# A streamed decode kernel: 256 more kept floats of W_q, a shorter weight ring in six places, eight loads fewer

## The chip, the cores and the metric

The kernel runs on one core of a Trainium2 chip. The metric is the time of one execution on the device in microseconds (us). A core has TensorE (PE, matmuls, its weight loads shown apart as PEld), VectorE (DVE), ScalarE (ACT), GpSimd (POOL) and SyncE (SP), which here does little else than issue the loads. Sixteen DMA engines move the data; every load from SP is cut by partition rows and spread over them.

## The reference

Two layers with the same weights, each of them an attention block and a gated block, on four tokens with 640 features:

```
W = 1024                                   # only the last 1024 cached positions
q = (layernorm(x) @ wq) in 32 heads of 128
p = softmax(q . k_cache[:, :, -W:] * 128**-0.5)
x = x + (p . v_cache[:, :, -W:]) @ wo
gate, up = layernorm(x) @ W_gate, layernorm(x) @ W_up      # 640 -> 1728
x = x + ((gate * (gate > 0)) * up) @ W_down
# all of it twice, the second time from the x of the first
```

All is float32. A layer reads about 168 MB of weights and cache (329,024 floats a partition).

## The kernel before, in words

**Data.** The host lays everything out as rows over 128 partitions. A size in this text is in floats a partition, so one unit is 512 bytes of a load over all partitions. There are four sources: `heads` (W_q, K, V and W_o of heads 0 to 26, in the order of use), `kept` (the same for heads 27 to 31, the groups K0 and K1), `mlp` (25,920 floats: W_gate, W_up and W_down) and `limbs` (512 columns of V of head 17, cut into pieces with few rows).

**Memory.** One big tile, `store`, has `STORE` floats a partition; beside it `first_q` holds the first `HELD` floats of `heads` from the start of the program to layer two, which so needn't load them again. In most of a layer the heads run through three places of `MOST` floats in `store` (`stretch`). Near the end of layer one `kept` fills the first `FRONT` = 47,360 floats, and its K, V, W_q and W_o stay there for layer two. Layer one's `mlp` has to pass through what is left: `f` (from `FRONT` to the end of `store`), and `a`, `k`, `q` (`AHEAD`, `BACK`, `AWAY`), which are parts of `kept` or of layer two's place that are moved away for that time: into `probs`, the two `pT` tiles and PSUM. The list `gu` says in which place each piece of `mlp` goes; this is the ring.

**Order.** `plan` is the list of all loads. `load()` issues from its front as long as the place of the next load is free (`live`); `done` and `free` mark places as free once the PE products that read them, or the copies that move them, are in the program. So all loads go through SP's one queue in a fixed order, and a load whose place isn't free yet holds up all that follow it. Limbs are loaded by L238 five or fewer rows at a time into the last `PART` floats of `store`.

**Computing.** Per layer: `normalized` and `deviation` (layer norm), then for each group of heads `query`, `scores`, `softmax`, `values`, `project`, where each product is one call of `product` (L276); then `forward`, which computes the gated block in the pieces `gate(j)`, `gated(j)`, `down(j)`. `busy(n)` and `fill(n)` (L358, L365) put products on PE whose results nobody reads; they do so only while `waits[0]` is true, and `normalized` sets it.

Of the kernel before, what the change touches and what calls it, by code (L numbers as in the profile page):

```python
# [13 lines left out]
B, D, H, DH, W, F = 4, 640, 32, 128, 1024, 1728  # L14
P = 128
# [11 lines left out]
KV = 4096  # L27
# [3 lines left out]
K0, K1 = N - 2, N - 1  # L31
KEPT = len(HEADS[K0]) + len(HEADS[K1])
# [25 lines left out]

HELD = 4608
STORE = 50304
FRONT = KEPT * 2 * (D + KV)


AHEAD = KEPT * D, KEPT * D + 1088
INSIDE = 864
BACK = FRONT - 2 * KV - 1728, FRONT - 2 * KV
AWAY = BACK[0] - 1280, BACK[0]
HOME = 12864  # L70
FIRST, MOST = 32128, 16064
LAP = 3 * MOST
SPLIT, PART = 17, 2048
LIMBS = [(half + i, 5, 0, 1536) for i in range(4) for half in (0, 32)] + [(i, 2, 1536, PART) for i in range(3)] + [(3, 1, 1536, PART), (7, 1, 1536, PART)]
RUNS = [(half, 20, 512 * s, 40 * s + 20 * (half > 0)) for s in range(3) for half in (0, 32)] + [(0, 8, 1536, 120)]


# [36 lines left out]
def decode_kernel(ctx: ExitStack, tc: tile.TileContext, x, source, out):  # L114
# [29 lines left out]
    def stretch(layer, lo, end, to):  # L144

        loads = []
        for hi in fewest(lo, end, -(-(end - lo) // MOST))[1]:
            if to + hi - lo > LAP:
                to = 0
            loads.append((lo, hi, to))  # L150
            to, lo = to + hi - lo, hi
        last = next(i for i, (lo, hi, _) in enumerate(loads) if lo < at_part("v", SPLIT) + KV - 512 <= hi)
        for i, (lo, hi, at) in enumerate(loads):
            if last - 3 < i <= last:
                half = (i - last + 1) * 6 + 1
                plan.extend((layer, "limbs", p, p + 1, STORE - PART) for p in range(max(half, 0), half + 6))
            put(layer, "heads", at, lo, hi)
        return to

# [16 lines left out]
    assert to <= KEPT * D or to > 2 * MOST, to  # L176
    put(0, "kept", KEPT * D, KEPT * D, q_end)
    put(0, "heads", q_end, turn, *mid, heads_end)
    put(0, "kept", k0, k0, k1, v0, v0 + 6656, v1, v1 + KV, v1 + 7168, FRONT)
    put(0, "kept", 0, 0, len(HEADS[K0]) * D, KEPT * D)  # L180


    f, z, a, q, k = FRONT, STORE - D, AHEAD[0], AWAY[0], BACK[0]
    assert STORE - FRONT == 1280 + 1024 + D
    gu = [(z, D), (f, 1280), (f + 1280, 1024), (a, 1088), (k, 960), (k + 960, 768), (q, 1280)]
    gu_end = [(f, 1280), (f + 1280, 1024), (z, D), (a, D + 256)]
    wd = [(k, 960), (k + 960, D), (q, 1280), *gu_end, (k, D), (k + D, D)]
    lo = 0
    for to, n in gu + gu + gu_end + wd:
        put(0, "mlp", to, lo, lo + n)  # L190
        lo += n
    assert lo == MLP


    lo = HELD
    for to, n in (f, 1280), (f + 1280, 1024), (z, D), (a, 1088), (k, 1728):
        put(1, "heads", to, lo, lo + n)
        lo += n
    to = AHEAD[1]
    for n in 832, 1280, 1024, 2048, 3392:  # L200
        to = put(1, "heads", to, lo, lo + n)
        lo += n
    assert to == HOME
# [47 lines left out]
    def place(layer, row, lo):  # L251

        if row == "heads" and lo < HELD:
            return first_q, lo, HELD - lo
        most = KV
        if row == "kept" and layer:
            if AHEAD[0] <= lo < AHEAD[1]:
                i = lo - AHEAD[0] - INSIDE
                if i < 0:
                    return probs, 1024 + i, -i  # L260
                return pT[i // P], GAP + i % P, min(P - i % P, AHEAD[1] - lo)
            if BACK[0] <= lo < BACK[1]:
                return store, HOME + lo - BACK[0], BACK[1] - lo
            most = min(x - lo for x in (AHEAD[0], BACK[0], FRONT) if x > lo)
        for first, m, p in held[key(layer, row)]:
            if first <= lo < first + m:
                return store, p + lo - first, min(first + m - lo, most)
        raise KeyError((layer, row, lo))
# [105 lines left out]
            nc.tensor.matmul(m[32 * g:32 * g + 32], sel_q, a, start=True, stop=True, tile_position=(0, 32 * g))  # L374
        return m

    def normalized():

        ysb, xc, sq = probs[:, :QUARTER], gates[:, :QUARTER], gates[:, QUARTER:2 * QUARTER]
        waits[0] = True  # L380
        nc.vector.tensor_reduce(su, y, axis=AX.X, op=ALU.add)
        nc.scalar.copy(ysb, y)
        busy(2)
        mu = mean(su)
        nc.vector.tensor_tensor(xc, ysb, mu.to_broadcast([P, QUARTER]), op=ALU.subtract)
# [77 lines left out]
    def values(layer, g, last=False):  # L463
# [30 lines left out]
        if last:  # L494
            waits[0] = layer == 0
            fill(1, pp[:, 0])
            nc.vector.tensor_copy(gates[:, 2 * P:], po[:, 2 * P:])  # L497
            nc.scalar.copy(gates[:, :2 * P], po[:, :2 * P])
            if layer == 0:
                nc.gpsimd.tensor_copy(pT[0][:, GAP:], store[:, AHEAD[0] + INSIDE:AHEAD[0] + INSIDE + P])  # L500
                rest = AHEAD[1] - AHEAD[0] - INSIDE - P
                nc.vector.tensor_copy(pT[1][:, GAP:GAP + rest], store[:, AHEAD[1] - rest:AHEAD[1]])
# [31 lines left out]

    def attention(layer):
        gs = order[layer]
        rstd = deviation(normalized())
        table(AF.Exp)
        query(layer, gs[0], True)
        if layer:  # L540
            for t in pT:
                nc.gpsimd.memset(t, 0.0)
        query_out(gs[0], rstd)
        query(layer, gs[1])
# [8 lines left out]
        for before, g, after, then in zip([None] + gs, gs, gs[1:] + [None], gs[2:] + [None] * 2):  # L553
            totals(g)
            turned()
            if layer == 0 and after is None:
                nc.scalar.copy(probs[:, QUARTER:], store[:, AHEAD[0]:AHEAD[0] + INSIDE])
                nc.scalar.copy(ps.rearrange("p j n -> p (j n)"), store[:, BACK[0]:BACK[0] + 1024])
                nc.scalar.copy(yy[:, QUARTER:3 * QUARTER], store[:, BACK[1] - 320:BACK[1]])
            if before is not None:  # L560
                values_turned(before)
            if then is not None and before is not None:
                query(layer, then)
                query_out(then, rstd)
# [18 lines left out]
        project(layer, gs[-1], True)  # L583

    def forward(layer):
        ss = normalized()
        gus, hTs = {}, {}

        def gate(j):
# [145 lines left out]
```

## Time and profile before

| | before |
|---|---|
| time, median of 3 runs | 729.77 us (729.51 to 730.13) |
| the profiled execution's own time | 729.74 us |
| its span, first to last instruction | 727.9 us |
| PE busy, DVE busy, ACT busy | 62%, 10%, 7% of the span |
| loads issued by SP | 93 (26 of them limbs) |
| bytes moved by the loads' queue | 310.37 MB in 13,392 packets |
| mean rate over the span | 427 GB/s |
| mean granted clock of TensorE | 0.815 of 2.4 GHz |

The profiled execution's time is 1.84 us more than its span; that part lies outside the instructions. The share of DMA is the mean over the sixteen engines, so 1.00 says that all of them had a packet under way all the time (packets overlap a little, so values just over 1 occur). The granted clock of PE has two levels, 1.2 and 2.4 GHz, shown as 0.50 and 1.00.

### The profile page before, as it was taken

Reading aid. Unit: us, or ns where it says so; the run is one execution under the profiler, and the core shown is the slowest. Engines: PE = TensorE matmul, PEld = TensorE weight load, DVE = VectorE, ACT = ScalarE, POOL = GpSimd, SP = SyncE. Lnnn points to the kernel's source line nnn. Section 1 sums busy time; section 2 is a strip of 40 time slices with the busy share of each in tenths; the row PEclk is TensorE's granted clock in tenths of the full one; section 3 lists DMA queues with packets and bytes.
Section 4 is the critical chain, followed back from the end, with each engine's and each line's share of the span. In section 5 each row is a group of like instructions: output and inputs, shape, how many; then the busy total and the mean of one; then the engine's idle time right before and its main releaser. Section 6 shows DMA issues by size and latency. Waiting matters only on the chain.

```text
span 727.9 us, 8368 instructions
## 1 busy us (share of the span) xinstructions
PE 450.0 (62%) x3824; PEld 146.9 (20%) x3824; DVE 70.5 (10%) x217; ACT 54.5 (7%) x102; POOL 2.4 (0%) x14
## 2 busy tenths in 40 slices
PE   3546565654645574619868896475756556558576
PEld 1111111111111121103334241021211012102123
DVE  2010001000010000001111211000000010001011
ACT  2000000000000000000412210000000000000100
POOL 0000000000000000000000000000000000000000
PEclk9567888887777787759999999677777878769989
DMA  9999999999999999999999999999999999999997
GB/s 409 444 394 447 440 444 434 412 435 444 443 428 416 421 457 418 444 422 426 418 414 412 426 431 452 429 441 433 434 423 440 438 436 417 441 444 423 425 420 312
DMA packets 13442, 310.91 MB, mean 427 GB/s; under 512 B 1576, under 2 KB 1916, under 8 KB 7136
## 3 DMA queue, kind: packets, MB, share of 16 engines
q1 hardware_dynamic: 13392, 310.37, 99.2%
q8 instruction: 30, 0.49, 0.2%
q14 instruction: 4, 0.03, 0.0%
q10 hardware_dynamic: 16, 0.01, 0.0%
HBM read 310.32 MB, written 0.05 MB: 426 GB/s over the span
## 4 chain that ended last, share of the span: by engine, by line
DMA 77%; PE 20%; DVE 1%; issue 1%; SPq 1%; ACT 0%; DVEq 0%; ACTq 0%
DMA store<-in_heads 62%; DMA store<-in_kept 9%; PE ps L276 8%; DMA store<-in_mlp 6%; PE po L276 6%; PE m L276 2%; PE y L276 1%; PE pp L276 1%; PE pp L461 1%; PE po L490 0%; PE m L432 0%; SPq L238 0%; PE po L358 0%; PE m L521 0%; PE m L512 0%
## 5 line engine op out<-in xcount | busy, mean ns | idle before, releaser
L276 PE MATMUL po<-store,pT 128*16 128x512 f32 x1026 | 157.9, 711 | 120.9 <-DMA store<-in_heads 115.2
L276 PE MATMUL ps<-store,qT 128*4 128x512 f32 (+2 forms) x998 | 152.7, 698 | 101.0 <-DMA store<-in_heads 80.7
L276 PEld LDWEIGHTS po<-store,pT 128*16 128x16 f32 x1026 | 33.4, 109 | 229.5 <-DMA store<-in_heads 126.7
L276 PEld LDWEIGHTS ps<-store,qT 128*4 128x4 f32 x998 | 30.8, 94 | 204.3 <-DMA store<-in_heads 91.8
L457 ACT ACTIVATE probs<-ps,nm 128x1024 f32<-128x1024 f32 x17 | 18.9, 1113 | 334.6 <-DVE nm L453 334.6
L453 DVE TENSOR_REDUCE nm<-ps 128x1 f32<-128x1024 f32 x17 | 20.8, 1225 | 233.9 <-PE ps L276 233.9
L276 PE MATMUL m<-store,xT 128*32 128x512 f32 (+3 forms) x146 | 27.9, 580 | 20.8 <-DMA store<-in_heads 20.8
L276 PE MATMUL y<-store,oT 128*4 128x160 f32 x512 | 23.2, 313 | 10.2 <-DMA store<-in_heads 8.9
L508 ACT COPY gates<-po 128x512 f32<-128x512 f32 x16 | 9.4, 586 | 256.5 <-PE po L276 256.5
L276 PE MATMUL pp<-store,xT 128*32 128x256 f32 (+2 forms) x320 | 20.3, 351 | 9.2 <-DMA store<-in_mlp 4.7
L470 DVE COPY pT<-pp 128x32 f32<-128x32 f32 x64 | 10.3, 184 | 143.5 <-PE po L276 126.4
L461 PE MATMUL pp<-sel_sb,probs 128*128 128x128 f32 x144 | 21.3, 297 | 0.0
L461 PEld LDWEIGHTS pp<-sel_sb,probs 128*128 128x128 f32 x144 | 18.7, 156 | 0.0
L514 DVE RECIPROCAL r<-m 128x16 f32<-128x16 f32 x18 | 4.6, 257 | 123.5 <-PE m L512 123.5
L276 PEld LDWEIGHTS y<-store,oT 128*4 128x4 f32 x512 | 12.7, 89 | 18.4 <-DMA store<-in_heads 9.2
L425 DVE TENSOR_SCALAR gates<-m,rstd 128x512 f32<-128x512 f32 (+2 forms) x18 | 12.4, 690 | 27.1 <-PE m L276 27.1
L276 PEld LDWEIGHTS pp<-store,xT 128*32 128x32 f32 x320 | 10.4, 109 | 17.7 <-DMA store<-in_mlp 8.5
L432 PE MATMUL m<-sel_sb,gates 128*128 128x128 f32 x64 | 12.7, 324 | 0.3 <-DVE gates L425 0.3
L276 PEld LDWEIGHTS m<-store,xT 128*32 128x32 f32 x146 | 6.0, 113 | 32.4 <-DMA store<-in_heads 23.3
L521 PE MATMUL m<-sel_sb,gates 128*128 128x128 f32 x72 | 11.9, 288 | 0.8 <-DVE gates L497 0.8
L432 PEld LDWEIGHTS m<-sel_sb,gates 128*128 128x128 f32 x64 | 7.9, 160 | 19.7 <-issue 18.9
L276 PE MATMUL y<-store,gates 128*4 128x160 f32 (+2 forms) x188 | 9.8, 296 | 1.7 <-DMA store<-in_mlp 1.1
(91 smaller groups left out, 135.7 us busy)
## 6 DMA issues: line engine op xcount, KB each, us to landing
store<-in_heads SPq DMA_DIRECT2D x15, 7936.0 KB
store<-in_heads SPq DMA_DIRECT2D x6, 8032.0 KB
store<-in_heads SPq DMA_DIRECT2D x2, 8000.0 KB
store<-in_heads SPq DMA_DIRECT2D x1, 7872.0 KB
store<-in_heads SPq DMA_DIRECT2D x1, 7424.0 KB
store<-in_heads SPq DMA_DIRECT2D x1, 7360.0 KB
store<-in_heads SPq DMA_DIRECT2D x1, 7168.0 KB
store<-in_heads SPq DMA_DIRECT2D x1, 6400.0 KB
```

The costliest lines, as they stand in the source:

```text
L276: nc.tensor.matmul(out[:, a:z], by, t[rows, p:p + z - a], start=start and not a, stop=stop and z == n, **how)
L425: nc.vector.tensor_scalar(gates[:, :len(HEADS[g]) * P], qp.pop(g), rstd, SCALE, op0=ALU.mult, op1=ALU.mult)
L432: nc.tensor.transpose(qt[:, i], gates[:, i * P:(i + 1) * P], ident)
L453: nc.vector.tensor_reduce(nm[g], to.rearrange("p j n -> p (j n)"), axis=AX.X, op=ALU.max, negate=True)
L457: nc.scalar.activation(probs, sc.pop(g).rearrange("p j n -> p (j n)"), AF.Exp, bias=nm.pop(g), accum_out=sums[g])
L461: nc.tensor.transpose(pp[:, c // 4, c % 4 * P:c % 4 * P + P], probs[:, c * P:(c + 1) * P], ident)
L470: nc.vector.tensor_copy(to, pp.rearrange("p j (c x) -> p (j c) x", c=4)[:, :, i:P:32])
L508: nc.scalar.copy(gates, po)
L514: nc.vector.reciprocal(r[g], so.rearrange("p (b i) -> p i b", b=B)[:, :SIDE])
L521: nc.tensor.transpose(ot[:, 127 * b:127 * b + P], gates[:, b * P:(b + 1) * P], ident)
```

## The change

- `HELD` grows from 4608 to 4864 floats: 256 more floats of W_q stay in `first_q` for layer two and are not loaded a second time. `STORE` shrinks by the same 256, to 50,048, and with it `MOST`, from 16,064 to 16,000.
- The ring of layer one's `mlp` is cut anew: 1280, 1408, 1152, 960, 768 and 1280 (6848 floats in six places) instead of 640, 1280, 1024, 1088, 960, 768 and 1280 (7040 in seven). The `mlp` takes 23 loads instead of 27, and layer two's first loads into the same places are four instead of five.
- `AHEAD` grows by 64 floats. What is moved out of it no longer fits in `probs` and the two `pT`: the last 32 floats go into `qT`, by a copy on POOL, and POOL clears `qT` as well in layer two before it's used again. The copy on DVE into the second `pT` is 128 floats wide instead of 96.
- The W_o of the kept heads comes in one load of 3200 instead of 1920 and 1280, and two of the kept V loads are 6144 and 6144 instead of 6656 and 5632.
- The limbs of a layer come in 12 loads instead of 13: the last 512 columns in four loads of two rows, instead of three of two and two of one. Six stand ahead of the load that brings head 17's V and six ahead of the load before that one; they were spread as 1, 6 and 6 over the last three such loads before.
- `normalized` gets an argument. The unread products are left out in the first layer norm of layer one and the second of layer two: in each of the two `busy(2)` and `fill(1)`, six products in all.

```diff
-HELD = 4608
-STORE = 50304
+HELD = 4864
+STORE = 50048
-AHEAD = KEPT * D, KEPT * D + 1088
+AHEAD = KEPT * D, KEPT * D + 1152
-FIRST, MOST = 32128, 16064
+FIRST, MOST = 32000, 16000
...
-            if last - 3 < i <= last:
-                half = (i - last + 1) * 6 + 1
+            if last - 2 < i <= last:
+                half = (i - last + 1) * 6
...
-    put(0, "kept", k0, k0, k1, v0, v0 + 6656, v1, v1 + KV, v1 + 7168, FRONT)
-    put(0, "kept", 0, 0, len(HEADS[K0]) * D, KEPT * D)
+    put(0, "kept", k0, k0, k1, v0, v0 + 6144, v1, v1 + KV, v1 + 7168, FRONT)
+    put(0, "kept", 0, 0, KEPT * D)
...
-    gu = [(z, D), (f, 1280), (f + 1280, 1024), (a, 1088), (k, 960), (k + 960, 768), (q, 1280)]
-    gu_end = [(f, 1280), (f + 1280, 1024), (z, D), (a, D + 256)]
-    wd = [(k, 960), (k + 960, D), (q, 1280), *gu_end, (k, D), (k + D, D)]
+    gu = [(f, 1280), (f + 1280, 1408), (a, 1152), (k, 960), (k + 960, 768), (q, 1280)]
+    wd = [*gu[:4], (k + 960, 704), (q, 1280), *gu[:4], (k + 960, D)]
...
-                return pT[i // P], GAP + i % P, min(P - i % P, AHEAD[1] - lo)
+                if i < 2 * P:
+                    return pT[i // P], GAP + i % P, P - i % P
+                return qT, i - 2 * P, AHEAD[1] - lo
...
-    def normalized():
+    def normalized(warm):
...
-        waits[0] = True
+        waits[0] = warm
...
-            for t in pT:
+            for t in qT, *pT:
                 nc.gpsimd.memset(t, 0.0)
...
+                lo = AHEAD[0] + INSIDE + 2 * P
+                nc.gpsimd.tensor_copy(qT[:, :AHEAD[1] - lo], store[:, lo:AHEAD[1]])
...
-        rstd = deviation(normalized())
+        rstd = deviation(normalized(layer > 0))
...
-        ss = normalized()
+        ss = normalized(layer == 0)
```

How the loads at the end of layer one's heads and in the first lap of the ring stand on SP (a name and `128x640` are the tile, the source, and partitions by floats). Before:

```order
L242 DMA store<-in_kept 128x1024
L242 DMA store<-in_kept 128x1920
L242 DMA store<-in_kept 128x1280
L242 DMA store<-in_mlp 128x640
L242 DMA store<-in_mlp 128x1280
L242 DMA store<-in_mlp 128x1024
L242 DMA store<-in_mlp 128x1088
L242 DMA store<-in_mlp 128x960
L242 DMA store<-in_mlp 128x768
```

And of the change, from the same load of the last kept V on:

```order
L241 DMA store<-in_kept 128x1024
L241 DMA store<-in_kept 128x3200
L241 DMA store<-in_mlp 128x1280
L241 DMA store<-in_mlp 128x1408
L241 DMA store<-in_mlp 128x1152
L241 DMA store<-in_mlp 128x960
L241 DMA store<-in_mlp 128x768
```

W_o is now one row, and the ring's first lap starts with 1280 floats in place of 640; ahead of the load into `a` (1088, now 1152) there are 2688 floats of `mlp` instead of 2944.

PE at the second layer norm of layer two (L374 is the mean over partitions, L358 and L365 are `busy` and `fill`, L276 the last of `project` and then `gate(3)`). Before:

```order
L276 MATMUL y<-store,oT 4x160 x12
L358 MATMUL po<-sel_sb 128x128 x2
L374 MATMUL m_123<-ones,sel_sb 32x1 x4
L365 MATMUL po<-sel_sb 128x128
L276 MATMUL pp<-store,xT 32x128 x15
L374 MATMUL m_124<-ones,sel_sb 32x1 x4
```

And of the change:

```order
L277 MATMUL y<-store,oT 4x160 x12
L375 MATMUL m_123<-ones,sel_sb 32x1 x4
L277 MATMUL pp<-store,xT 32x128 x15
L375 MATMUL m_124<-ones,sel_sb 32x1 x4
L405 MATMUL y<-probs,sel_sb 128x160
```

The three unread products are gone; what is read stands in the same order.

## Rows read from the trace of the kernel before

**Rows 1.** The page: span; the loads' queue (packets, MB, share of 16 engines' span).

```profile
span 727.9 us, 8368 instructions
...
q1 hardware_dynamic: 13392, 310.37, 99.2%
```

**Rows 2.** The chain that ended last, in order of time, from 690 us on.

```profile
693.76 30.76 DMA store<-in_mlp
...
724.57 0.45 PE y L276 x6
```

**Rows 3.** Windows: start:end, length, PE busy (instructions), PE clock, DMA share, GB/s.

```profile
60.00:340.00 280.00, 156.02 (x1198) 0.78 1.00 431
366.00:390.00 24.00, 18.00 (x254) 1.00 1.02 414
390.00:394.00 4.00, 4.00 (x58) 1.00 1.01 393
394.00:405.00 11.00, 9.98 (x130) 1.00 1.02 406
```

**Rows 4.** Windows of the last microseconds, the same columns.

```profile
721.50:722.50 1.00, 0.79 (x24) 1.00 0.89 351
722.50:723.50 1.00, 0.55 (x20) 1.00 0.57 215
723.50:724.50 1.00, 0.93 (x24) 1.00 0.35 112
```

**Rows 5.** Timeline of SP: start, us, line, instruction, count.

```profile
216.11 3.35 SPq L238 DMA_DIRECT2D store<-in_limbs  x6
...
345.69 42.93 SPq L242 DMA_DIRECT2D store<-in_mlp  x27
```

**Rows 6.** Timeline at the start: issue of the first load, first use.

```profile
0.73 0.38 SPq L229 DMA_DIRECT2D first_q<-in_heads  x1
...
8.63 3.98 PE L276 MATMUL m<-first_q,xT 128*32 128x512 f32 x24 [2.66 <-DMA first_q<-in_heads]
```

**Rows 7.** The chain from 336 to 400 us, in order of time.

```profile
340.57 22.62 DMA store<-in_kept
...
369.66 6.99 DMA store<-in_mlp
...
377.38 7.58 DMA store<-in_mlp
```

**Rows 8.** Timeline of PE from 361.5 to 366 us: kept W_o, then the first gate.

```profile
361.71 1.00 PE L276 MATMUL y<-store,oT 128*4 128x160 f32 x24
...
363.34 0.73 PE L276 MATMUL y<-store,oT 128*4 128x160 f32 x16 [0.21 <-DMA store<-in_kept]
...
365.79 0.42 PE L276 MATMUL pp<-store,xT 128*32 128x128 f32 x6 [0.47 <-DVE xT L388]
```

**Rows 9.** Waits from 362 to 398 us: total, times, longest.

```profile
PE pp L276 <- DMA store<-in_mlp: 4.7, 9, 1.1
```

**Rows 10.** Groups by line: busy, mean ns, idle time before and its releaser.

```profile
L542 POOL MEMSET pT<- 128x140 f32 x2 | 0.4, 214 | 41.3 <-PE m L276 41.3
L500 POOL COPY pT<-store 128x128 f32<-128x128 f32 x1 | 0.3, 290 | 353.9 <-DMA store<-in_kept 353.9
L502 DVE COPY pT<-store 128x96 f32<-128x96 f32 x1 | 0.2, 199 | 0.0
```

**Rows 11.** Windows on PE's clock, columns as in rows 3.

```profile
449.60:452.60 3.00, 0.00 (x0) 1.00 1.08 461
453.00:455.00 2.00, 0.00 (x0) 0.50 1.35 584
706.00:718.00 12.00, 9.16 (x168) 1.00 0.99 421
```

**Rows 12.** Timeline of PE near the end.

```profile
718.57 0.84 PE L276 MATMUL y<-store,probs 128*4 128x160 f32 x16 [1.19 <-DMA store<-in_mlp]
...
721.71 1.00 PE L276 MATMUL y<-store,gates 128*4 128x160 f32 x24 [1.10 <-DMA store<-in_mlp]
```

More of the change, by code (lines that the diff above doesn't have):

```diff
@@ L70 @@
 HOME = 12864
-FIRST, MOST = 32128, 16064
+FIRST, MOST = 32000, 16000
 LAP = 3 * MOST
 SPLIT, PART = 17, 2048
-LIMBS = [(half + i, 5, 0, 1536) for i in range(4) for half in (0, 32)] + [(i, 2, 1536, PART) for i in range(3)] + [(3, 1, 1536, PART), (7, 1, 1536, PART)]
+LIMBS = [(half + i, 5, 0, 1536) for i in range(4) for half in (0, 32)] + [(i, 2, 1536, PART) for i in range(4)]
 RUNS = [(half, 20, 512 * s, 40 * s + 20 * (half > 0)) for s in range(3) for half in (0, 32)] + [(0, 8, 1536, 120)]
@@ L153, in stretch @@
         for i, (lo, hi, at) in enumerate(loads):
-            if last - 3 < i <= last:
-                half = (i - last + 1) * 6 + 1
-                plan.extend((layer, "limbs", p, p + 1, STORE - PART) for p in range(max(half, 0), half + 6))
+            if last - 2 < i <= last:
+                half = (i - last + 1) * 6
+                plan.extend((layer, "limbs", p, p + 1, STORE - PART) for p in range(half, half + 6))
             put(layer, "heads", at, lo, hi)
@@ L178, in decode_kernel @@
     put(0, "heads", q_end, turn, *mid, heads_end)
-    put(0, "kept", k0, k0, k1, v0, v0 + 6656, v1, v1 + KV, v1 + 7168, FRONT)
-    put(0, "kept", 0, 0, len(HEADS[K0]) * D, KEPT * D)
-    f, z, a, q, k = FRONT, STORE - D, AHEAD[0], AWAY[0], BACK[0]
-    assert STORE - FRONT == 1280 + 1024 + D
-    gu = [(z, D), (f, 1280), (f + 1280, 1024), (a, 1088), (k, 960), (k + 960, 768), (q, 1280)]
-    gu_end = [(f, 1280), (f + 1280, 1024), (z, D), (a, D + 256)]
-    wd = [(k, 960), (k + 960, D), (q, 1280), *gu_end, (k, D), (k + D, D)]
+    put(0, "kept", k0, k0, k1, v0, v0 + 6144, v1, v1 + KV, v1 + 7168, FRONT)
+    put(0, "kept", 0, 0, KEPT * D)
+    f, a, q, k = FRONT, AHEAD[0], AWAY[0], BACK[0]
+    assert STORE - FRONT == 1280 + 1408
+    gu = [(f, 1280), (f + 1280, 1408), (a, 1152), (k, 960), (k + 960, 768), (q, 1280)]
+    wd = [*gu[:4], (k + 960, 704), (q, 1280), *gu[:4], (k + 960, D)]
     lo = 0
-    for to, n in gu + gu + gu_end + wd:
+    for to, n in gu + gu + wd:
         put(0, "mlp", to, lo, lo + n)
@@ L195, in decode_kernel @@
     lo = HELD
-    for to, n in (f, 1280), (f + 1280, 1024), (z, D), (a, 1088), (k, 1728):
+    for to, n in (f, 1280), (f + 1280, 1408), (a, 1152), (k, 1728):
         put(1, "heads", to, lo, lo + n)
@@ L199, in decode_kernel @@
     to = AHEAD[1]
-    for n in 832, 1280, 1024, 2048, 3392:
+    for n in 768, 1280, 1024, 2048, 3392:
         to = put(1, "heads", to, lo, lo + n)
@@ L499, in values @@
             if layer == 0:
-                nc.gpsimd.tensor_copy(pT[0][:, GAP:], store[:, AHEAD[0] + INSIDE:AHEAD[0] + INSIDE + P])
-                rest = AHEAD[1] - AHEAD[0] - INSIDE - P
-                nc.vector.tensor_copy(pT[1][:, GAP:GAP + rest], store[:, AHEAD[1] - rest:AHEAD[1]])
+                for i, on in enumerate([nc.gpsimd, nc.vector]):
+                    lo = AHEAD[0] + INSIDE + P * i
+                    on.tensor_copy(pT[i][:, GAP:], store[:, lo:lo + P])
                 free(*AHEAD)
```

## The prediction, made before the change was run

> **What bounds the kernel now.** I read the page's head first. The loads' queue carries 310.37 MB and its packets fill 99.2% of sixteen engines' span of 727.9 us [rows 1]. So the kernel is a stream of loads, and the reader should ask three things only: how many bytes, at what rate, and does the stream ever stand still. The rate comes from windows: 431 GB/s over 280 us of large loads, 414 GB/s in the 24 us of layer one's ring, where loads are small [rows 3]. The share of DMA there is 1.02, as full as elsewhere, so the lower rate is a price of small loads and not a standstill. The thinnest stretch is 390 to 405 us, where layer one's MLP ends and layer two begins: 393 and 406 GB/s. Last, the chain in order of time: from 693.76 us it is one row, 30.76 us of `mlp` loads, up to the last six products [rows 2]. PE waits for loads in the ring (4.7 us in nine waits [rows 9]) and near the end (1.19 and 1.10 us [rows 12]). What shortens the stream shortens the time; what shortens PE does not.
>
> **The change part by part.** The sum is made against the profiled execution's 729.74 us (span 727.9 and 1.84 around it), which stands 0.03 us under the median of 729.77.
>
> *256 floats kept.* They are 256 x 512 = 131,072 bytes that layer two doesn't load. At 431 GB/s that is 0.30 us. First_q is 256 floats longer at the start, so the first product comes 0.30 us later than its 8.63 us [rows 6]; the stream doesn't wait for it, because the loads behind it are already issued.
>
> *Six full loads fewer* (four of `mlp`, one of layer two's first, one of W_o), with the same bytes. The 27 `mlp` loads [rows 5] carry 25,920 floats, so a mean one has 960 floats or 491,520 bytes. In 24 us at 414 GB/s 9.94 MB pass, 20.2 loads; at 431 GB/s they would take 23.05 us. The 0.95 us between are 47 ns a load. Bounds: from below nothing, if the lower rate has to do with something else in that stretch; from above 2.43 us, which is what a load costs beyond its bytes when it finds the queue empty: the first one, issued at 0.73 us and used at 8.63 [rows 6], takes 7.90 us for 2.36 MB, of which 5.47 are its bytes at 431 GB/s. I take 47 ns, because the share of 1.02 says that the ring's loads did not find an empty queue: six make 0.28 us.
>
> The Trainium skill has a rule that would make this term the whole change: DMA: Bandwidth & Descriptors (Anatomy of one DMA) gives each DMA a fixed cost of about 2.0 us plus its bytes at 436 GB/s. By it the six loads would be an estimated 12 us and the time about 717. The page says that this cost is mostly completion latency; the 47 ns above agree with that reading, since a full queue hides it.
>
> *Two limb loads fewer*, with the same bytes. Six of them take SP 3.35 us to issue [rows 5], 0.56 each, under a load of 16,000 floats that keeps the stream busy for 19 us (8.2 MB at 431). On the stream they cost at most the 47 ns of a full load each. I take 0.05 us for both, bounds 0 and 0.09. The sixteen engines don't end together: their share falls to 0.89, 0.57 and 0.35 in the last three microseconds [rows 4], which is 0.11 + 0.43 + 0.65 = 1.2 us of idle on average; the time is set by the latest engine. Loads of five, two or one rows can't fill sixteen engines, so which engine gets their rows matters, and the change moves two rows a layer, of 2 KB each. At 1/16 of 431 GB/s such a row is 0.08 us of one engine: between -0.16 and +0.16 us on the latest one. I take 0.
>
> *A ring of 6848 floats in six places.* The stream would stop if the queue ran dry. How far is it from that? A load issued at 369.66 us is landed 6.99 us later, one at 377.38 after 7.58 [rows 7]. They are small pieces (the first is 1088 floats, 1.35 us at 414 GB/s), so with the 2.43 us of an empty queue 6.99 - 1.35 - 2.43 = 3.2 us of other data lay ahead. The ring is 192 floats shorter (0.24 us at 414 GB/s), and a place comes free up to 320 floats later (1408 instead of 1088: 0.40 us). 3.2 - 0.64 leaves 2.6 us. Cost: 0. If the cover were gone, it would be 0.64 us for each of the 3.8 laps.
>
> *W_o in one load: a new wait.* PE projects the first kept heads at 361.71 and the others at 363.34, just as each load has landed [rows 8]; the second landed at 363.20 [rows 7]. With one load both wait for about 363.2. The two together, 1.00 + 0.73 us and a product of `fill` between them, then end near 365.3 and not at 364.07, 1.2 us later. Behind them in PE's queue wait the layer norm and `gate(3)`, which frees the ring's first place; that place has 1280 floats now, so it needs ten products and not five. `gate(3)` started at 365.79 [rows 8] and will start near 367.0, and its ten products take about a microsecond (six passes took 0.42, and a product is two): the place is free at 368.0. All six places were issued by then, 8.5 us of data at 414 GB/s counted from 363.2, so the queue lasts until 371.7, 3.7 us more, where the next load needs up to 2.43. So 1.3 us are left: hidden, but this is the closest call of all. PE itself makes it up, since it waits 4.7 us for loads right behind [rows 9].
>
> *Copies and clears.* The copy on DVE (199 ns for 96 columns) grows by about 30 ns; the copy of 32 floats on POOL and the clearing of `qT` are each under the 290 and 214 ns of their larger neighbours [rows 10], and POOL had waited 353.9 and 41.3 us ahead of those. The load into `a` is held back by 30 ns at most; hidden by the same queue, 0.03 us if not.
>
> *Six unread products fewer.* PE waits for loads soon after in both places; no term. What they might do is keep PE's clock up, see the rivals.
>
> Sum: 0.30 + 0.28 + 0.05 = 0.63 us; 729.74 - 0.63 = 729.11. **729.1 us**, 0.09% less than before. By the bounds of the terms: from 728.6 (0.30, 0.56 with twice the price per load, 0.09 and 0.16 gained) to 729.6 (0.30 gained for the bytes, nothing for the loads, 0.16 lost on the latest engine).
>
> **The rivals.** What this kernel's measurement can tell from no change is about 0.2%, 1.5 us.
>
> *Slower: the queue runs dry in the first lap.* Place: behind kept W_o. For it: three delays fall together there (1.2 for W_o, half a microsecond for five more products, 0.24 for the ring), and between 390 and 405 us the stream is already below the 414 GB/s of the ring. Against it: the 1.3 us left above, and a share of DMA that nowhere falls under 1.00 [rows 3]. It decides once the lead that I worked out as 3.7 us is really under 2.43. If nothing of it were there, the first lap would lose the three delays, 1.9 us, and the 2.8 others 0.64 each: 729.1 + 1.9 + 1.8 = 732.8 us. Chance 0.05.
>
> *Slower: PE's clock falls in layer two's MLP.* It fell to 1.2 GHz at about 453 us, after PE had done nothing for three microseconds [rows 11]. Without the three products PE has little to do during the layer norm ahead of 706 us. If it then ran at 1.2 GHz from 706 to 718, its 9.16 us of work would take 18.3; 2.84 idle and 2.29 of waits for loads [rows 11, 12] absorb 5.1 of the 9.2, and the end comes 4.0 us later, 733.1. It decides below a mean clock of about 0.64 in that window. Against it: that layer norm takes less than two microseconds and has the means over partitions in it, and waits of 1.19 and 1.10 us near the end left the clock at 1.00. Chance 0.02.
>
> *Faster: a load costs what a lone one costs.* 6 x 2.43 = 14.6 us for the six, and 714.8 with the bytes. Against it: 20.2 loads in 24 us at 2.43 each beyond their bytes would have left 49 us of gaps in a stretch whose share is 1.02. Chance 0.01. (It is the mechanism of the rule of the Trainium skill's page DMA: Bandwidth & Descriptors, above.) *Faster: the engines end more together.* If all of the 1.2 us of idle at the end [rows 4] went with the moved rows, the time would be 727.9; from 0.83 us on it passes 0.2%. But the rows moved are worth 0.16. Chance 0.04.
>
> *The change does nothing measurable for the stream:* 729.8. It lies within my forecast of no change.
>
> **How the numbers follow.** Within 0.2%: 0.88, with 729.1 as its likeliest. Faster 0.05, slower 0.07. The range holds the bounds of the sum, 728.6 to 729.6, with 0.3 to 0.5 us on either side for the spread of runs (729.51 to 730.13 before): 728.3 to 730.1. It reaches neither the dry queue nor the fallen clock, which hold less than 2 in 10.
>
> **What the profile after would show.** Right: the queue moves 310.24 MB, with 131,072 bytes less read; a window of the ring shows a rate above 414 GB/s, near 418; DMA's share stays near 1.02 from 362 to 390 us and at 1.00 or above up to 405; the last `mlp` load lands about 0.6 us earlier than 724.52. PE's two projects of kept W_o run back to back from about 363. Wrong: a window between 364 and 405 us with a share well under 1.0 (the ring ran dry), a granted clock of 0.50 after 704 us, or waits of PE for loads that end later than the sum says. The weakest step is the lead in the first lap; the price per load is the most uncertain term.

## The result, and the profile after

The changed kernel takes 734.04 us (median of 7 runs, 730.67 to 735.07) beside 729.70 of the kernel before (7 runs, 729.43 to 730.13): 1.005 times as long, 95% interval 1.0035 to 1.0065. It is slower by 4.3 us, where 0.6 us less was forecast. The runs also lie 4.4 us apart, and those of the kernel before 0.7.

The profiled execution took 735.07 us; it is the slowest of the seven. Its page shows the bytes that the prediction named, in fewer packets, with a lower share (span; the loads' queue with packets, MB and share of 16 engines' span; compare [rows 1]):

```profile
span 733.2 us, 8350 instructions
...
q1 hardware_dynamic: 12528, 310.24, 98.7%
```

So the stream is as short as promised and stands still more. Where? Windows over the ring and the layer turn (start:end, length, PE busy (instructions), PE clock, DMA share, GB/s), to be laid beside [rows 3]:

```profile
362.00:366.00 4.00, 2.88 (x38) 0.67 1.00 409
366.00:370.00 4.00, 3.40 (x65) 0.90 0.94 382
370.00:374.00 4.00, 2.73 (x50) 1.00 0.89 261
...
394.00:398.00 4.00, 4.00 (x64) 1.00 0.89 315
398.00:402.00 4.00, 3.28 (x68) 1.00 0.89 318
...
362.00:410.00 48.00, 39.24 (x495) 0.93 0.98 379
```

Two holes: one behind kept W_o (370 to 374), one at the turn from layer one to layer two (394 to 402). The kernel before over the same 48 us:

```profile
362.00:410.00 48.00, 39.03 (x512) 1.00 1.02 414
```

So 48 x (414 - 379) / 414 = 4.1 us of transfer are missing. Note how little of it the share of DMA tells: 0.98 over the whole stretch.

What PE did ahead of the first hole, in its timeline (start, us, line, operation, count, idle time before and its releaser), which answers to [rows 8]:

```profile
363.12 1.59 PE L277 MATMUL y<-store,oT 128*4 128x160 f32 x24 [1.32 <-DMA store<-in_kept]
...
365.36 1.25 PE L277 MATMUL y<-store,oT 128*4 128x160 f32 x16
...
368.35 1.18 PE L277 MATMUL pp<-store,xT 128*32 128x128 f32 x27 [0.46 <-DVE xT L389]
```

PE waited for the whole of W_o, as foreseen, but its clock fell just behind that wait (0.59 from 363.1 to 364.7 us, 0.50 from there to 366.6), and the two projects took 1.59 and 1.25 us where they had taken 1.00 and 0.73. `gate(3)` starts at 368.35, 2.56 us later than at 365.79; 1.2 were forecast.

The end of the kernel is another matter. A window and the timeline of PE in layer two's MLP:

```profile
706.00:718.00 12.00, 9.70 (x122) 0.59 1.00 429
```

```profile
712.98 4.50 PE L277 MATMUL pp<-store,xT 128*32 128x256 f32 x40 [0.43 <-DVE gates L609]
...
718.53 3.94 PE L277 MATMUL pp<-store,xT 128*32 128x256 f32 x40 [0.53 <-DVE probs L609]
...
723.35 2.37 PE L277 MATMUL pp<-store,xT 128*32 128x256 f32 x40 [0.88 <-DVE probs L609]
```

The same forty products take 4.50, 3.94 and then 2.37 us: the first at the lower of the clock's two levels (1.2 GHz), the second nearly all at it, the third at 2.4. So PE, not the stream, is last: the chain that ended last has no load in it after 697.67 us and ends in

```profile
730.47 0.33 DVE first_q L680
```

where that of the kernel before was one row of loads up to the last six products [rows 2].

The copies and clears, which the prediction put at nothing, stayed small (groups by line and form, answering to [rows 10]): the copy on DVE grew from 199 to 217 ns, 18 where about 30 were forecast, and the new copy takes 209 ns on a POOL that had waited 342 us.

```profile
L503 DVE COPY pT<-store 128x128 f32<-128x128 f32 x1 | 0.2, 217 | 0.0
L560 POOL COPY qT<-store 128x32 f32<-128x32 f32 x1 | 0.2, 209 | 342.1 <-PE ps L277 342.1
```

### The profile page after: what moved, and what is told of

The parts are those of the page before. It is cut to its first block, busy times and chain, and to the rows that moved or that the text cites. A ratio compares the mean times of both kernels' runs of the same rounds, so it can differ in the third digit from the quotient of the medians.

```text
span 733.2 us, 8350 instructions
## 1 busy us (share of the span) xinstructions
PE 449.6 (61%) x3820; PEld 148.6 (20%) x3820; DVE 70.5 (10%) x217; ACT 54.5 (7%) x102; POOL 2.7 (0%) x16
## 4 chain that ended last, share of the span: by engine, by line
DMA 70%; PE 26%; another core or an unknown queue 1%; DVE 1%; issue 1%; ACT 0%; SPq 0%; DVEq 0%; ACTq 0%
DMA store<-in_heads 59%; DMA store<-in_kept 9%; PE ps L277 8%; PE po L277 7%; PE pp L277 3%; PE y L277 3%; DMA store<-in_mlp 2%; PE m L277 1%; PE pp L462 1%; PE m L433 1%; PE po L491 0%; PE m L522 0%; PE po L366 0%; PE po L359 0%
## 5 line engine op out<-in xcount | busy, mean ns | idle before, releaser
L277 PE MATMUL po<-store,pT 128*16 128x512 f32 (+2 forms) x1028 | 157.1, 714 | 134.6 <-DMA store<-in_heads 127.8
L277 PE MATMUL ps<-store,qT 128*4 128x512 f32 (+5 forms) x996 | 149.0, 668 | 99.7 <-DMA store<-in_heads 78.3
L277 PE MATMUL pp<-store,xT 128*32 128x256 f32 (+2 forms) x316 | 25.3, 428 | 9.1 <-DMA store<-in_mlp 4.7
L462 PEld LDWEIGHTS pp<-sel_sb,probs 128*128 128x128 f32 x144 | 18.2, 153 | 0.0
L277 PEld LDWEIGHTS pp<-store,xT 128*32 128x32 f32 x316 | 12.3, 130 | 19.6 <-DMA store<-in_mlp 7.8
L277 PE MATMUL y<-store,gates 128*4 128x160 f32 (+3 forms) x188 | 8.9, 296 | 0.5 <-DVE first_q L627 0.5
```

What stands on the lines that cost most here:

```text
L277: nc.tensor.matmul(out[:, a:z], by, t[rows, p:p + z - a], start=start and not a, stop=stop and z == n, **how)
L462: nc.tensor.transpose(pp[:, c // 4, c % 4 * P:c % 4 * P + P], probs[:, c * P:(c + 1) * P], ident)
```

## The experiments

Three theories stood at the start. **A**: the wait for the whole of W_o makes PE late, its clock falls, and the ring runs dry in the first lap and again at the layer turn. **B**: the products on the identity that nothing reads had kept PE's clock up in layer two's MLP (three of the six that are left out stand ahead of it, at layer two's second layer norm); without them PE ends after the loads. **C**: the smaller ring of larger places costs time by itself. All times below are medians; "rate" is GB/s from 362 to 410 us in the profiled execution, and ratios are to the kernel before on the same chip.

| kernel | us (lowest to highest, runs) | ratio, 95% | rate |
|---|---|---|---|
| before (in six measurements) | 729.51 to 729.71 | | 414 |
| after | 734.04 (730.67 to 735.07, 7) | 1.0050 (1.0035 to 1.0065) | 379 |
| two_wo | 730.71 (730.19 to 733.25, 12) | 1.0018 (1.0010 to 1.0027) | 405 |
| warm | 732.65 (731.46 to 732.94, 5) | 1.0034 (1.0022 to 1.0046) | 385 |
| two_warm | 730.55 (729.60 to 731.52, 11) | 1.0010 (1.0001 to 1.0018) | 405 |
| before_cold | 729.64 (729.39 to 729.87, 11) | 0.9998 (0.9989 to 1.0007) | 414 |
| before_one_wo | 730.51 (729.49 to 735.42, 11) | 1.0023 (1.0007 to 1.0039) | 410 |
| one_wo_fill | 731.94 (731.45 to 732.37, 5) | 1.0032 (1.0020 to 1.0045) | 393 |
| turn | 730.76 (730.12 to 731.24, 11) | 1.0016 (1.0007 to 1.0024) | 406 |
| lean | 729.96 (729.60 to 731.30, 11) | 1.0008 (0.9999 to 1.0017) | 414 |
| lean_turn | 730.74 (729.68 to 731.75, 11) | 1.0013 (1.0004 to 1.0021) | 398 |
| lean_seven | 730.40 (729.66 to 731.04, 11) | 1.0006 (0.9997 to 1.0015) | 413 |
| lean_none | 730.15 (729.31 to 731.94, 11) | 1.0009 (1.0000 to 1.0018) | 414 |
| before_lean | 729.64 (729.47 to 730.68, 11) | 1.0000 (0.9992 to 1.0009) | 413 |
| lean_fill | 732.57 (730.99 to 735.53, 6) | 1.0046 (1.0029 to 1.0063) | 397 |
| none_fill | 732.56 (730.93 to 735.92, 6) | 1.0045 (1.0030 to 1.0061) | 386 |
| one_lean_fill | 733.88 (732.17 to 734.53, 5) | 1.0054 (1.0041 to 1.0066) | 373 |
| one_fill_cut | 731.59 (731.03 to 734.64, 12) | 1.0031 (1.0021 to 1.0040) | 388 |
| after_cut | 732.89 (731.17 to 733.10, 5) | 1.0037 (1.0024 to 1.0050) | 382 |
| lean_cut | 730.15 (729.91 to 730.61, 11) | 1.0005 (0.9997 to 1.0014) | 413 |

### W_o in two loads again: two_wo

```diff
-    put(0, "kept", 0, 0, KEPT * D)
+    put(0, "kept", 0, 0, len(HEADS[K0]) * D, KEPT * D)
```

> The change with kept W_o in two loads again (1920 and 1280); all else as changed. Theory A (the queue runs dry in the ring's first lap because one W_o load holds PE back and lets its clock fall): the share of DMA from 366 to 374 us is back at 1.0 or above, and about 3.5 us come back, 730.5 us where the clock still falls in layer two's MLP and 729.1 where it doesn't. Theory B (the time is lost only in layer two's MLP, to PE's clock): 734.0, as changed. Theory C (the ring of six larger places runs dry by itself): 733 to 734, with the dry stretch still there.

730.71 us: this one load is worth 3.3 of the 4.3 us by the medians. That 730.5 had been expected for a fallen clock in layer two is luck: what is left has another cause, as follows. Windows of it, columns as above:

```profile
370.00:374.00 4.00, 2.46 (x31) 1.00 1.01 397
...
394.00:398.00 4.00, 3.28 (x61) 1.00 0.91 336
398.00:402.00 4.00, 3.63 (x48) 1.00 0.98 376
...
706.00:718.00 12.00, 9.69 (x136) 0.72 0.99 421
```

The first hole is gone (397 instead of 261), the second is smaller and stays. PE's clock fell in layer two here too, but it was back sooner: 0.72 over the window, and only the first forty products are slow, as the timeline shows:

```profile
710.71 3.60 PE L277 MATMUL pp<-store,xT 128*32 128x256 f32 x40 [0.43 <-DVE gates L609]
...
715.20 2.37 PE L277 MATMUL pp<-store,xT 128*32 128x256 f32 x40 [0.55 <-DVE probs L609]
```

The chain that ended last (start, us, what) is a row of loads up to the last six products, so the fall cost nothing in this execution:

```profile
694.83 30.45 DMA store<-in_mlp
725.33 0.45 PE y L277 x6
```

### The three products of layer two back: warm, and both: two_warm

```diff
-        ss = normalized(layer == 0)
+        ss = normalized(True)
```

(The three products in the first layer norm of layer one stay out.)

> The change with the three unread products of layer two's second layer norm put back; W_o in one load as changed. Theory A: the last load still lands near 728 us and the end follows it by 0.9 us as before instead of 2.3, so about 732.6 us. Theory B: 729.1 us. Theory C: 732.6, as A.

> Both put back: W_o in two loads and the three unread products; the ring of six places, the 256 kept floats and the limbs as changed. Theories A and B together: 729.1 us in every run, as the prediction's sum has it, 0.6 below the kernel before. Theory C: 732 or more, with a share of DMA below 0.95 somewhere between 366 and 402 us.

warm takes 732.65 us, 1.4 less than the changed kernel; the clock holds, and the last load is followed by six products again. two_warm takes 730.55, only 0.16 less than two_wo. The time of two_warm is a miss: 729.1 had been expected from A and B together.

B is borne out by the profiles: with the three products the clock is 1.00 from 706 to 718 us in warm and in two_warm, without them 0.59 and 0.72. Its price of 1.4 us is a difference of medians whose ranges overlap. The price is larger than with two loads of W_o because the clock stayed low longer in the changed kernel's profile, and not because PE came late to layer two's MLP: `gate(3)` starts there at 707.04 us in two_wo, 18.2 us before the last load is in, and at 709.31 in the changed kernel, where bytes still land from 728.0 to 728.3 us (13 GB/s, then nothing for 0.3 us), so some 18.7 us before. Why the clock came back sooner in one of them, no run shows. Windows of warm:

```profile
370.00:374.00 4.00, 3.40 (x58) 1.00 0.97 371
374.00:378.00 4.00, 3.37 (x36) 0.70 1.02 406
...
394.00:398.00 4.00, 3.96 (x61) 1.00 0.89 300
...
706.00:718.00 12.00, 9.44 (x168) 1.00 1.00 426
```

Its timeline at W_o holds a surprise. After the same wait, of 1.33 us, the clock did not fall; `gate(3)` starts 1.18 us late, and 371 GB/s say that the queue ran dry even so. (The clock fell later, to 0.70 from 374 to 378 us and 0.60 from 386 to 390, and the turn is as dry as in the changed kernel.)

```profile
363.17 1.00 PE L277 MATMUL y<-store,oT 128*4 128x160 f32 x24 [1.33 <-DMA store<-in_kept]
...
366.97 1.18 PE L277 MATMUL pp<-store,xT 128*32 128x128 f32 x27 [0.46 <-DVE xT L389]
```

### Two edits alone on the kernel before: before_cold, before_one_wo

before_cold leaves the six products out of the kernel before; before_one_wo has its W_o in one load:

```diff
-    put(0, "kept", 0, 0, len(HEADS[K0]) * D, KEPT * D)
+    put(0, "kept", 0, 0, KEPT * D)
```

> The kernel before with the six unread products left out and nothing else changed. Theory B: PE's granted clock falls to 0.50 behind the layer norm at 705 us in some executions, and those end up to 1.5 us later, 729.7 to 731.2, spread wider than the 0.7 us of the kernel before. Theories A and C have nothing to say here: 729.7 if the products do nothing.

> The kernel before, with the kept W_o of layer one in one load instead of two; all else as before. Theory A (the wait for the whole of W_o, with the clock that falls in it, makes PE late and lets the queue run dry in the first lap) holds for the ring of seven places too: the gate's first product of layer one at about 368 us instead of 365.79, GB/s under 400 somewhere in 366 to 402, and 731 to 732.5 us, 1.3 to 2.8 us above the kernel before (729.67). Rival, the late gate costs something only together with the ring of larger places (theory C): within 0.5 us of the kernel before.

before_cold is unchanged, 729.64. before_one_wo loses 1.0 us in the median, and three of its 11 runs are at 732.4, 734.1 and 735.4. In its profiled execution (730.25 us) PE is 1.2 us late at a full clock, as its timeline shows:

```profile
363.16 1.00 PE L276 MATMUL y<-store,oT 128*4 128x160 f32 x24 [1.33 <-DMA store<-in_kept]
...
366.97 1.18 PE L276 MATMUL pp<-store,xT 128*32 128x128 f32 x27 [0.47 <-DVE xT L388]
```

And a window of it:

```profile
370.00:374.00 4.00, 3.79 (x58) 1.00 1.00 394
```

394 GB/s, where the changed kernel's ring gives 371 for the same lateness: in these executions the old ring nearly covers it, the new one doesn't. The three slow runs left no profile.

### The wait without the clock: one_wo_fill

In the changed kernel, with the products of layer two's MLP back:

```diff
             free(*AWAY)
+            fill(5)
             project(layer, gs[-2])
...
+        ss = normalized(True)
```

> The changed kernel with W_o in one load, the products on the identity in layer two's last stage back, and five more of them put where PE waits for that load, so that PE is not idle there. It parts the wait from the clock. If the clock's fall is most of theory A's loss: the granted clock stays 1.00 from 362 to 370 us, the gate's first product comes near 367 us instead of 368.35, and the time is 730.5 to 731.2 us, near the kernel with W_o in two loads (730.55). If the wait itself is enough to dry the queue: 731.8 to 732.7 us, near the same kernel without the five (732.65), with GB/s under 380 in 370 to 374 or 394 to 402.

Its timeline of PE at W_o:

```profile
361.71 1.38 PE L366 MATMUL po<-sel_sb 128*128 128x128 f32 x10
363.29 1.00 PE L277 MATMUL y<-store,oT 128*4 128x160 f32 x24 [0.19 <-DMA store<-in_kept]
...
367.10 1.18 PE L277 MATMUL pp<-store,xT 128*32 128x128 f32 x27 [0.47 <-DVE xT L389]
```

And the window of the first lap:

```profile
370.00:374.00 4.00, 3.40 (x57) 1.00 0.98 368
374.00:378.00 4.00, 2.73 (x40) 1.00 1.01 397
```

731.94 us. The clock is 1.00 throughout, the gate is 1.3 us late, and the ring is dry at 370 to 374. The wait by itself, with the five products in it, costs 1.4 us (730.55 to 731.94); what I had taken for most of A, the clock, adds the rest where it falls (0.7 from 731.94 to warm's 732.65, whose ranges overlap).

### What is left at the layer turn: turn, lean, lean_none, before_lean

two_warm still loses 9 of 414 GB/s over 48 us, 1.0 us, all of it at 394 to 402 (356 GB/s, 407 before). turn refills smaller pieces there; lean lets PE reach the turn sooner:

```diff
-    for to, n in (f, 1280), (f + 1280, 1408), (a, 1152), (k, 1728):
+    for to, n in (f, 704), (f + 704, 1024), (f + 1728, 960), (a, 1152), (k, 1728):
```

```diff
-                elif not (last and f > 1):
+                elif f % 2 and not (last and f > 1):
                     busy(1)
```

> The kernel with W_o in two loads and the products on the identity back (two_warm), and layer two's first heads loads cut 704, 1024, 960, 1152, 1728 instead of 1280, 1408, 1152, 1728, at the places where the last products of layer one end; one load more (0.05 us). Theory C (what is left of the loss is the larger places at the layer turn, each of which is refilled only when its last product is done): GB/s in 394 to 402 back over 390, and 729.2 to 729.8 us. Rival, the places are late because PE is late there, however they are cut, and the ring is 256 floats smaller: GB/s under 360 in 394 to 398 still, and 730.4 to 730.8 us.

> The kernel with W_o in two loads and the products on the identity back (two_warm), with only every other one of the single products on the identity between the pieces of layer one's W_down; 5 fewer, some 0.26 us of PE each, so the end of layer one on PE up to 1.2 us earlier. If PE's pace at the layer turn is what lets the places come free late: y of layer one done near 394.5 us instead of 395.65, GB/s in 394 to 402 over 390, 729.2 to 729.9 us. Rival, PE only waits for the next load sooner: no change, 730.4 to 730.7 us. Rival, the clock falls for want of those products, as in layer two's last stage of the changed kernel: granted clock 0.50 somewhere in 388 to 400, 731.5 us or more.

turn changes nothing measurable (730.76), but its windows show that it did something: the hole is gone from 394 to 402 us and stands at 402 to 406, where the kernel before moved 410 GB/s:

```profile
394.00:398.00 4.00, 3.28 (x59) 1.00 1.02 401
...
402.00:406.00 4.00, 4.00 (x40) 1.00 0.98 346
```

Smaller pieces put the hole off and do not fill it. lean takes 729.96, and its profiled execution 729.60, the fastest of its eleven, with the turn at the rate of the kernel before, as its windows show:

```profile
394.00:398.00 4.00, 3.28 (x66) 1.00 1.03 403
398.00:402.00 4.00, 3.63 (x41) 1.00 1.01 409
...
362.00:410.00 48.00, 38.88 (x501) 1.00 1.02 414
```

So what counted at the turn was PE's pace through layer one's W_down more than how the loads were cut. That is read from the windows; in the time, lean and two_warm can hardly be told apart (1.0008 and 1.0010, with intervals that overlap almost wholly). Leaving all of those products out is no better, and the kernel before gains nothing by lean (729.64): its turn is already full. That its longer ring is what covers PE's pace is argued; no run keeps the rest of the change and puts the old ring back.

> As lean, but none of the single products on the identity between the pieces of layer one's W_down is left. PE is at the end of layer one up to 1 us earlier than with lean if loads don't hold it: 729.5 to 730.0 us, no better than lean, if the queue is full there already. Rival, the clock falls for want of them: granted clock 0.50 somewhere in 388 to 400 and 730.5 us or more.

> The kernel before with only every other one of the single products on the identity between the pieces of layer one's W_down, and nothing else. In its own trace the layer turn moved 393 GB/s in 390 to 394, 0.2 us' worth: 729.3 to 729.5 us if PE's pace there costs it that; 729.5 to 729.7, no change, if its ring of 7040 floats in seven places covers that pace; 730.5 or more if the clock falls for want of those products.

### Trying to hold it: lean_turn, lean_seven, lean_fill, none_fill, one_lean_fill

lean's runs still reach 731.30. lean_turn has both edits above; lean_seven cuts the ring's first place into two halves of 640 in every lap; lean_fill and none_fill (on lean and lean_none) put two products on the identity behind each fifth of the gate products of blocks 1 and 2, against a falling clock; one_lean_fill does the same on one_wo_fill, with lean's edit.

```diff
                     done(layer, "mlp", lo, 2 * n)
+                if layer == 0 and 0 < j < 3:
+                    fill(2)
```

> Both the fewer products between the pieces of layer one's W_down (lean) and the finer first loads of layer two (turn). If the two take away what is left of the dry queue at the layer turn: every run near the best of lean, 729.3 to 729.7 us median and none over 730.3, GB/s over 395 in all of 390 to 406. Rival, the first lap of the ring (370 to 374) is dry in some runs as well and neither change reaches it: 729.8 to 730.2 us, with single runs over 731.

> Lean, and the first place of 1280 floats in two halves of 640 in each lap of layer one's MLP: seven places again, but 6848 floats, three loads more (0.14 us). If the size of the places in the first lap is what is left (a place comes free only with its last product, and the lap's first is awaited most): 729.2 to 729.6 us and no run over 730.3. If the floats count and not the places: 729.9 to 730.4 us, as lean with three loads more.

> Lean, with two more products on the identity after each fifth of layer one's gate products of blocks 1 and 2, where PE waits for loads (20 in all). If the clock's falls in those waits make the scatter: granted clock 1.00 in every window of 370 to 398, no run over 730.3, median 729.2 to 729.6 us. If the smaller ring's margin is spent whatever the clock: 729.9 to 730.3 us, scatter up to 731 as lean.

> The same, with none of the single products on the identity in layer one's W_down (as lean_none, whose runs went from 729.31 to 731.94). If the clock makes the scatter and the products in the gate's waits hold it: 729.2 to 729.6 us, no run over 730.3. If W_down without them lets the clock fall by itself: 730 us or more, with the fall after 388 us.

> W_o in one load, with five products on the identity in its wait (one_wo_fill, 731.94), and both of PE's changes of lean_fill. If the wait of 1.2 us by itself dries the ring: GB/s under 385 in 370 to 374 and 730.4 us or more, at least 0.8 above lean_fill. If the wait costs only by PE being late at the layer turn: within 0.4 us of lean_fill.

None of them is better than lean. lean_turn's profiled execution (731.45) fell into the case that lean avoids: PE's clock fell ahead of the turn, and the turn was dry (windows of it):

```profile
382.00:386.00 4.00, 2.10 (x22) 0.75 1.01 408
...
394.00:398.00 4.00, 3.55 (x52) 1.00 1.03 333
398.00:402.00 4.00, 3.33 (x53) 1.00 0.91 326
```

I took the scatter for the clock's doing, and lean_fill says that a dry turn doesn't need it: its profiled execution has the clock at 1.00 from 362 to 410 us and takes 731.85. The products that keep the clock also keep PE from catching up. `down(3)` starts at 387.62 us in the timeline of lean_fill:

```profile
387.62 0.46 PE L277 MATMUL y<-store,probs 128*4 128x160 f32 x10
```

In that of lean it starts at 385.51:

```profile
385.51 0.62 PE L277 MATMUL y<-store,probs 128*4 128x160 f32 x10
```

The two microseconds come back as a dry turn, in a window of lean_fill:

```profile
398.00:402.00 4.00, 3.08 (x51) 1.00 0.97 361
```

A late PE is enough; the clock is one way among others to make it late. Nor did the products always keep the clock: it is 0.58 from 374 to 378 us in none_fill's profile, and 0.50 from 398 to 402 in one_lean_fill's, with 284 GB/s there.

### Why the first lap has no lead: one_fill_cut, after_cut, lean_cut

The next three ask why a wait of 1.2 us dries a lap that was to have 1.3 us left after it. In the kernel before, SP issues two loads while `gate(3)` runs (SP's timeline from 366 to 368.9 us: start, us, instruction, count):

```profile
366.46 1.00 SPq L242 DMA_DIRECT2D store<-in_mlp  x2
```

In two_warm it issues one:

```profile
366.80 0.33 SPq L241 DMA_DIRECT2D store<-in_mlp  x1
```

`gate(3)` reads 5 x 3 x 128 = 1920 floats. The old ring's first two places, 640 and 1280, end at 1920; the new ones end at 1280 and 2688, so 640 floats that are read can't be refilled before `gate(0)`. I cut the second lap's loads there:

```diff
-    for to, n in gu + gu + wd:
+    for to, n in gu + [(f, 1280), (f + 1280, 640), (f + 1920, 768)] + gu[2:] + wd:
```

> one_wo_fill (W_o in one load, five products on the identity in its wait, 731.94 us) with the second lap's first two loads, 1280 and 1408 floats, cut as 1280, 640 and 768, so that what gate(3) has read, 1920 floats, can be refilled at once; one load more. If the cut of the places is why the first lap runs dry: SP issues two loads at 368.2 us, GB/s in 370 to 374 at 395 or more instead of 368, and 730.5 to 731.2 us. If the wait of 1.2 us alone dries the queue: GB/s there under 380 and 731.7 to 732.2 us.

> The changed kernel (734.04 us) with that cut alone. If the cut is the larger part of the first lap's loss: GB/s in 370 to 374 over 340 instead of 261, and 1 to 2 us less, 732 to 733 us; what is left is the clock, the layer turn and layer two's last stage. If the clock and the wait are: 733.5 us or more.

> lean (W_o in two loads, the products on the identity back in layer two's last stage, half of the single ones in layer one's W_down left out; 729.96 us, runs to 731.3) with that cut. If lean's worse runs come from the first lap: median 729.2 to 729.5 us, no run over 730.2, which beats the kernel before by 0.1 to 0.4 us. If they come from the layer turn: no change, 729.8 to 730.2 with runs over 731.

In one_fill_cut SP issues both together, in the same stretch of its timeline:

```profile
368.06 0.80 SPq L241 DMA_DIRECT2D store<-in_mlp  x2
```

And where one_wo_fill moves 368 and then 397 GB/s, it moves 399 and then 381, as windows of it show:

```profile
370.00:374.00 4.00, 3.25 (x57) 1.00 1.00 399
374.00:378.00 4.00, 2.91 (x46) 1.00 1.03 381
```

So where the places end is why the wait of 1.2 us dried 370 to 374; about half of the gain there is lost again by 378. The time follows little, 731.59 after 731.94, with overlapping runs, and misses the 731.2 or less that was expected: in its profiled execution the clock fell afterwards (0.66 at 382 to 386) and the turn was dry (315 GB/s at 398 to 402). after_cut gains 1.1 us (732.89), as expected, but not for the reason expected. PE is as late there as in the changed kernel (its clock fell at W_o too), and the first lap is no fuller, as windows of after_cut show (261 and 387 GB/s in the changed kernel; over 340 in the first was expected):

```profile
370.00:374.00 4.00, 2.71 (x49) 1.00 0.88 291
374.00:378.00 4.00, 2.75 (x36) 1.00 0.95 330
```

What differs is its end: the clock in layer two held better (0.86 instead of 0.59 from 706 to 718), and the chain that ended last ends on the loads. lean_cut, at 730.15, is no better than lean. No kernel here beats the one before.

## Why the prediction was wrong, point by point

*W_o in one load: a new wait* is the step that failed, and the closest call turned out the wrong way. It said 1.2 us later, "1.3 us left: hidden". The 1.2 holds where the clock holds (366.97 in warm, 367.0 forecast), and SP issues the first place again at 368.19 in one_wo_fill (368.0 forecast). Three things were wrong in what came after. The lead was counted to the refill of the first place, as if the rest followed at once; but the second load came at 370.45 us, two microseconds later, because its place's end at 2688 lies beyond the 1920 floats that `gate(3)` reads (cut at 1920 in one_fill_cut, it came with the first), and 370 to 374 us moved 368 GB/s. With the clock at 1.00 the wait cost 1.4 us and not nothing (two_warm to one_wo_fill). The clock can fall behind that wait, and then the lateness is 2.56 us; the prediction weighed the clock in layer two only. And "PE itself makes it up, since it waits 4.7 us for loads right behind" [rows 9] is no comfort: a PE that frees its places late has later loads to wait for, and the same 4.7 us stand in the trace of after. Its lateness came back at the layer turn (342 GB/s from 394 to 402 us in one_wo_fill, 356 in two_warm).

*A ring of 6848 floats in six places* was put at 0 with 2.6 us left. That lead was worked out in the first lap. At the layer turn there is none: two_warm loses 1.0 us there (405 for 414 GB/s). It differs from the kernel before in more than the ring, so that the ring is the cause is argued. The row was in hand: 393 GB/s at 390 to 394 [rows 3]. The prediction named it as the thinnest stretch, but had ruled out a standstill in the ring because the share was 1.02. In these traces the share is a bad witness: 331 GB/s in two_warm, 330 in one_wo_fill and 333 in lean_turn, all at 394 to 398, stand beside shares of 0.97, 1.00 and 1.03.

*Six unread products fewer* was no term, and its danger was a rival with a chance of 0.02. The mechanism was right and the bound agrees with both profiles: it was to decide below a mean clock of 0.64 from 706 to 718 us; the changed kernel had 0.59 there and ended on PE, two_wo had 0.72 and ended on the loads. It was to cost 4.0 us more, with the clock at 0.50 throughout, and cost 1.4 (734.04 to 732.65); at 0.59 the prediction's own sum gives 9.16 / 0.59 - 9.16 - 5.1 = 1.3. What was wrong is the chance: it leant on waits of 1.19 and 1.10 us that had left the clock at 1.00, and such a wait says little (below).

*The rival of the dry queue*, with a chance of 0.05, gave 732.8 us; warm, which has that loss and not the other, takes 732.65. That they are so near is luck: the rival put 1.9 us on the first lap and spread 1.8 over the others for the shorter ring, while in warm's profile 370 to 374 us lose 0.3 us and 390 to 402 lose 2.5. The two rivals were weighed as if only one could come; in the changed kernel's profile both did.

*256 floats, six loads, two limb loads*: 0.63 us in sum. The bytes are as forecast. For the time, take the profiled execution of each of the 15 kernels with the change's bytes that ended on the loads, and add back what the rate of the table says is lost, 48 x (414 - rate) / 414: two_warm 730.76 - 1.04 = 729.72, warm 732.94 - 3.36 = 729.58, one_wo_fill 731.94 - 2.43 = 729.51, lean 729.60. They run from 729.15 to 730.34 with a median of 729.59, beside 729.74 of the kernel before. The gain was near 0.15, and single values run from 0.6 gained to 0.6 lost; the 47 ns for each load can't be made out, and lean's ring moves 415 GB/s from 366 to 390 us, not 418. The rule of the Trainium skill that was weighed there (DMA: Bandwidth & Descriptors, Anatomy of one DMA: about 2.0 us fixed for each DMA, which that section gives for DMAs issued by GpSimd, and here SP issues them), by which six loads fewer are an estimated 12 us, is not borne out for a full queue: no median with the fewer loads is under that of the kernel before.

The same sum checks the account of the changed kernel: 735.07 - 4.06 = 731.01, 1.4 above 729.59, and 1.4 is what the clock in layer two cost by warm.

What stays open: which run meets a falling clock, and when the clock comes back, and so the scatter. lean_fill shows that PE's lateness is enough without it, not that the clock has no part.

## What to carry to other kernels

Read a dry queue from GB/s against a neighbour with loads of the same size, not from the share of busy time. In a ring, work out the lead at the place where the consumer is latest (here a layer norm and the turn of a layer), and lay the ends of its places on the ends of the groups that the consumer reads; a larger place than that is a smaller ring (here the better ends filled a window, and the times hardly followed). A lateness of the consumer isn't made up by the waits behind it where its pace is near that of the loads, and products that keep the clock up cost where they sit in that path.

## What the runs showed that I had not expected

The share of DMA hides a queue that runs dry: the layer turn moved 300 GB/s at a share of 0.89 (warm) and 333 at 1.03 (lean_turn), both at 394 to 398 us, where the kernel before moved 406 at 1.02.

The same wait did different things to PE's clock: after a wait of 1.32 us ahead of the same products it fell to 0.50 in the changed kernel, and after 1.33 us it stayed at 1.00 in warm and before_one_wo. The products on the identity went without loss from the kernel before (before_cold, clock 1.00 from 706 to 718 us) and not from the changed one (0.59). A single profile in which the clock held is no evidence that it holds.

A kernel whose queue is at the edge shows it in its spread before it shows in its best run: lean_none has the best run with the change, 729.31 us, and another of 731.94.
